# Later weight loads, paced behind compute, and LayerNorm statistics regrouped in a two-layer spectral-filter and MLP kernel

## Chip, cores, metric

One core of one Trainium2 chip. The metric is the device time of one execution in microseconds (us). PE is TensorE, DVE VectorE, ACT ScalarE, SP SyncE, POOL GpSimd. The profiles of before and after are of the fastest execution that each has (832.4 us before).

## The reference

Abridged: casts and batch handling are left out.

```python
def _A_ref(x, w_r, w_i):                       # spectral filter: B, S, D = 1, 2048, 576
    X = rfft2(x.astype(float32), axes=(-2, -1))
    X = X * (w_r + 1j * w_i)                   # w_r, w_i: 2048 x 289
    return irfft2(X, s=(S, D)).astype(bfloat16)

def _B_ref(x, w1, b1, w2, b2):                 # MLP: 576 -> 4608 -> 576
    h = gelu(einsum("bsd,df->bsf", layernorm(x), w1) + b1)
    return einsum("bsf,fd->bsd", h, w2) + b2

x = A_x
x = x + _A_ref(layernorm(x), A_w_r, A_w_i)
x = x + _B_ref(layernorm(x), B_w1, B_b1, B_w2, B_b2)
x = x + _A_ref(layernorm(x), A_w_r, A_w_i)     # the same weights again
x = x + _B_ref(layernorm(x), B_w1, B_b1, B_w2, B_b2)
```

## The kernel before

The transforms are matrix products. Per 128-row tile, stage A does fold, turn (transpose), `dft_d`, `dft_v`, then an "exchange": a DMA from SBUF to SBUF that spreads one tile over other partitions. A stage that follows needs all 16 exchanges. In the profiles, psb and pss are tiles in PSUM, where PE writes; xT, z and y1 (shown as y) are the tile after `turn`, `dft_d` and `dft_v`; v_sb, b_sb, r_sb and h_sb are large buffers in SBUF that the stages take turns in. w2 lies in v_sb and r_sb, w1 in w_sb, the GELU results in h_sb, and between two MLPs the spectral weights and the inverse transform i1 in h_sb too.

```python
    def exchange(dst, slot, src):                       # 145 KB, on SP's queue
        p0 = 32 * (slot // 4) + slot % 4
        ins = nc.sync.dma_start(out=dst[p0 : p0 + 29 : 4], in_=src).ins
        # ... (cut: declared independent of the other exchanges)

        def dft_v(self, t, on_act):
            # ... (cut: four matmuls into py)
            y1 = work.tile([P, 2, KP], BF16, tag="y1", bufs=3)
            if on_act:
                nc.scalar.copy(out=y1[:], in_=py[:, :, 0:KP])
            else:
                nc.vector.tensor_copy(out=y1[:], in_=py[:, :, 0:KP])
            exchange(self.vx, t, y1[:])

        def run_all(self):                              # stage A
            for i in range(NT + 3):
                if 0 <= i - 3 < NT:
                    self.dft_v(order[i - 3], on_act=(i % 2 == 0))
                if 0 <= i - 2 < NT:
                    self.dft_d(order[i - 2])            # PE, then z on ACT, scaled by rs
                if 0 <= i - 1 < NT:
                    self.turn(order[i - 1])             # PE, then xT on ACT
                if i < NT:
                    self.fold(order[i])                 # DVE
                    if i < 4:
                        self.stats([order[i]])          # LayerNorm statistics, DVE and a root on ACT
                    elif i % 4 == 0:
                        self.stats(order[i : i + 4])

    vx, hx = at(v_sb, [P, 16, 2, KP]), at(b_sb, [P, 16, 2, KP])
    wks, i1s = middle_tiles()             # in h_sb, with a GpSimd memset
    middle_loads(wks, i1s, True)          # f2, spectral weights, i1: issued at once
    mlp_const_loads()                     # constants, w1 (4.6 MB), w1r: issued at once
    SpectralIn(vx, sqrt=True).run_all()
    for li in range(N_LAYERS):
        last = li == N_LAYERS - 1
        middle(vx, hx, wks, i1s)
        if li == 0:
            load_w2((0, 1, 2, 3))         # 5.2 MB, as soon as v_sb and r_sb are free
            # ... (cut)
        else:
            load_w2((2, 3))
        prep = Prep(0, sqrt=li == 0)      # Newton steps on DVE where sqrt is False
        spectral_out(hx, prep)
        # ... (cut: second MLP, w2 groups 0 and 1)
            mlp(li, prep, SpectralIn(vx, sqrt=False))
            wks, i1s = middle_tiles()
            middle_loads(wks, i1s, False)
```

## Time and profile before

| | before |
|---|---|
| time, median | 836.2 us (832.4 to 838.0, 16 runs) |
| span of the profiled execution | 830.6 us |
| PE busy | 750.9 us, 90% |
| stages A to H | 72.2, 35.2, 33.3, D and E together 330.4, 28.5, 35.4, 295.6 us |

The two page lines on which the theory rests are the DMA share of 40 equal slices (in tenths) and what the engines moved, kernel before:

```profile
DMA  9951640000000000000001644300000000000000
GB/s 299 350 131 52 189 159 1 1 1 8 15 1 8 17 8 1 8 15 8 1 8 51 171 110 148 115 1 1 22 8 1 8 23 0 2 15 16 1 8 22
```

A slice is 20.8 us: the first two are saturated with loads and lie wholly in stage A.

### The profile page before, as it was taken

How to read it: one execution, taken by the hardware profiler on the slowest of the kernel's cores; microseconds unless marked ns; L12 is line 12 of the kernel's file. 1: busy time of each engine (PE TensorE's matmuls, PEld its weight loads, DVE VectorE, ACT ScalarE, POOL GpSimd, SP SyncE). 2: the span in 40 equal slices, each digit the busy share in tenths (PEclk: the TensorE clock that was granted, in tenths of full speed). 3: DMA queues.
4: the chain of work that ended last, by engine and by line, in shares of the span. 5: the costliest groups of instructions: out<-in, count | busy, mean ns of one | idle time of the engine just before them, and what ended most of it. 6: DMA issues, size and time to landing. Idle time of an engine off the chain costs nothing.

```text
span 830.6 us, 12285 instructions
## 1 busy us (share of the span) xinstructions
PE 750.9 (90%) x5121; PEld 460.9 (55%) x5121; DVE 275.4 (33%) x905; ACT 331.7 (40%) x514; POOL 37.5 (5%) x61
## 2 busy tenths in 40 slices
PE   6556569999999999999999477999999999999998
PEld 4334245358636853784378245535853773585376
DVE  6334559204611460242024476920140122020001
ACT  5435534642354235424532274354035205502510
POOL 6300000000000000000002200000000000000000
PEclk9868889999999999999999698899999999999999
DMA  9951640000000000000001644300000000000000
GB/s 299 350 131 52 189 159 1 1 1 8 15 1 8 17 8 1 8 15 8 1 8 51 171 110 148 115 1 1 22 8 1 8 23 0 2 15 16 1 8 22
DMA packets 18504, 41.59 MB, mean 50 GB/s; under 512 B 1796, under 2 KB 12880, under 8 KB 17936
## 3 DMA queue, kind: packets, MB, share of 16 engines
q0 software_dynamic: 6464, 27.88, 10.7%
q1 hardware_dynamic: 11584, 12.46, 5.3%
q8 instruction: 40, 0.66, 0.3%
q10 hardware_dynamic: 400, 0.47, 0.2%
q14 instruction: 16, 0.13, 0.0%
HBM read 28.93 MB, written 2.36 MB: 38 GB/s over the span
## 4 chain that ended last, share of the span: by engine, by line
PE 78%; DVE 10%; DMA 9%; ACT 2%; issue 1%; SPq 0%; DVEq 0%; ACTq 0%
PE psb L510 34%; PE psb L484 31%; DMA v_sb<-y 5%; PE psb L490 5%; PE psb L289 2%; DMA b_sb<-r_sb 2%; DVE tt L432 2%; PE psb L396 1%; DVE r_sb L359 1%; DVE r_sb L360 1%; DVE x_sb L433 1%; PE pss L472 1%; DVE x_sb L434 1%; DVE stats L234 1%; DVE r_sb L361 1%
## 5 line engine op out<-in xcount | busy, mean ns | idle before, releaser
L484 PE MATMUL psb<-yT,w_sb 128*128 128x512 bf16 x1152 | 261.2, 380 | 1.7 <-DVE x_sb L434 1.0
L510 PEld LDWEIGHTS <-h_sb 128*128 128x128 bf16 x2304 | 223.1, 98 | 58.2 <-issue 3.4
L497 ACT ACTIVATE h_sb<-psb,b_sb 128x512 bf16<-128x512 f32 x288 | 174.5, 688 | 197.1 <-PE psb L490 197.1
L484 PEld LDWEIGHTS <-w_sb 128*128 128x128 bf16 x1152 | 107.3, 98 | 148.8 <-issue 28.8
L510 PE MATMUL psb<-r_sb,h_sb 128*128 128x288 bf16 x1280 | 168.9, 286 | 0.0
L510 PE MATMUL psb<-v_sb,h_sb 128*128 128x288 bf16 x1024 | 133.7, 286 | 0.0
L518 DVE TENSOR_TENSOR x_sb<-psb,xb 128x576 bf16<-128x576 f32 x32 | 24.2, 758 | 259.7 <-PE psb L510 259.7
L462 DVE TENSOR_SCALAR xn<-x_sb,mv,rs 128x576 bf16<-128x576 bf16 x32 | 13.9, 433 | 195.0 <-PE pss L472 138.8
L474 ACT COPY yT<-pss 128x640 bf16<-128x640 bf16 x32 | 22.1, 692 | 71.3 <-PE pss L472 71.3
L234 DVE BATCH_NORM_STATS2 stats<-x_sb 128x6 f32<-128x288 bf16 x128 | 50.5, 436 | 0.0
L490 PE MATMUL psb<-yT,w1r_sb 64*128 64x512 bf16 x288 | 43.6, 381 | 0.0
L294 ACT ACTIVATE z<-psb,rs 128x580 bf16<-128x580 f32 x32 | 29.4, 917 | 35.2 <-PE psb L289 33.3
L281 ACT COPY xT<-pss 96x768 bf16<-96x768 bf16 x32 | 25.1, 785 | 43.7 <-PE pss L279 43.7
L289 PE MATMUL psb<-c_fd,xT 96*128 96x290 bf16 x192 | 35.2, 327 | 2.3 <-ACT xT L281 2.3
L310 ACT CAST y<-psb 128x580 bf16<-128x580 f32 x24 | 15.4, 642 | 50.1 <-PE psb L307 33.4
L426 PE MATMUL psb<-c_gd,u 128*128 128x288 bf16 x128 | 26.8, 302 | 8.2 <-ACT u L401 5.4
L432 DVE TENSOR_TENSOR tt<-psb,x_sb 128x576 f32<-128x576 f32 x32 | 24.0, 751 | 25.1 <-PE psb L426 24.8
L304 PE MATMUL psb<-z,c_k 128*128 128x290 bf16 x32 | 9.9, 311 | 23.4 <-ACT z L294 23.4
L371 PE MATMUL psb<-r_sb,h_sb 128*128 128x290 bf16 x128 | 23.9, 298 | 6.4 <-DVE r_sb L361 3.1
L289 PEld LDWEIGHTS <-xT 96*128 96x128 bf16 x192 | 20.2, 110 | 12.7 <-ACT xT L281 5.2
L350 ACT CAST r_sb<-psb 128x580 bf16<-128x580 f32 x32 | 20.8, 649 | 14.0 <-PE psb L348 12.7
L373 ACT CAST r_sb<-psb 128x580 bf16<-128x580 f32 x32 | 20.6, 644 | 13.9 <-PE psb L371 7.0
(75 smaller groups left out, 509.5 us busy)
## 6 DMA issues: line engine op xcount, KB each, us to landing
r_sb<-in_B_w_dram POOLq DMA_DIRECT2D x4, 1440.0 KB, 8.2
w_sb<-in_B_w_dram POOLq DMA_DIRECT2D x4, 1152.0 KB, 14.2
v_sb<-in_B_w_dram POOLq DMA_DIRECT2D x4, 1152.0 KB, 8.7
h_sb<-const_i POOLq DMA_DIRECT2D x8, 384.0 KB, 8.9
v_sb<-y SPq DMA_DIRECT2D x16, 145.0 KB
b_sb<-r_sb SPq DMA_DIRECT2D x16, 145.0 KB
b_sb<-y SPq DMA_DIRECT2D x16, 145.0 KB
v_sb<-r_sb SPq DMA_DIRECT2D x16, 145.0 KB
```

The source lines that it names most:

```text
L234: nc.vector.bn_stats(out=stats[:, h, :], in_=x_sb[:, t, h * DH : (h + 1) * DH])
L281: nc.scalar.copy(out=xT[:], in_=pt[0:96])
L289: nc.tensor.matmul(pz[:, o, 0:KP], lhsT=xT[:, 3 * o + ci, :], rhs=c_fd[:, 3 * o + ci, :], start=(ci == 0), stop=(ci == 2),)
L294: nc.scalar.activation(out=z[:].rearrange("p r (j o) -> p r o j", o=2), in_=pz[:, :, 0:KP].rearrange("p o (r j) -> p r o j", r=2), func=AC ...
L371: nc.tensor.matmul(ph[:, o, 0:KP], lhsT=i1[:, n % 4, pl, :], rhs=xp[:, ri, :], start=(q == 0), stop=(q == 1))
L426: nc.tensor.matmul(po[:, o, 0:DH], lhsT=lhsT, rhs=c_gd[0 : (98 if q == 2 else 128), 3 * o + q, :], start=(q == 0), stop=(q == 2),)
L432: nc.vector.tensor_tensor(out=tt[:], in0=po[:, 0:1, 0:DH].to_broadcast([P, 2, DH]), in1=xr, op=ALU.add)
L484: nc.tensor.matmul(phs[q // 2][:, q % 2, :], lhsT=w1_sb[:, ci, (fg + q) * 128 : (fg + q + 1) * 128], rhs=yT[:, ci, :], start=(ci == 0), st ...
L490: nc.tensor.matmul(phs[q // 2][:, q % 2, :], lhsT=w1r_sb[rows, (fg + q) // 2, :], rhs=yT[rows, 4, :], start=False, stop=True,)
L497: nc.scalar.activation(out=ht[:], in_=phs[q // 2][:, q % 2, :], func=ACT.Gelu_apprx_tanh, bias=b1_sb[:, fc : fc + 1], scale=1.0)
L510: nc.tensor.matmul(po[:, h, 0:DH], lhsT=hts[fc][:, i * 128 : (i + 1) * 128], rhs=w2_chunk[fc][:, h * DH : (h + 1) * DH], start=(fc == 0), ...
L518: nc.vector.tensor_tensor(out=xr, in0=po[:, :, 0:DH], in1=xb[:], op=ALU.add)
```

## The change

Its intent: keep bulk loads from competing with exchanges, by loading each tensor only shortly before it is needed and tying each load to an instruction that marks progress; and take small waits out of the statistics. In stage E an extra root on a constant (`warm`) brings ACT's table in early.

```diff
+    def load(out, in_, behind=None):
+        ins = nc.gpsimd.dma_start(out=out, in_=in_).ins
+        if behind is not None:
+            tc.add_manual_dep(ins, marks[behind].name, SYNC, reason="pace of the loads")
 ...
-            nc.gpsimd.memset(wk[:, :, :, KP - 1 : KP], 0.0)      # in both layers
+        nc.vector.memset(wk[:, :, :, KP - 1 : KP], 0.0)          # once
 ...
-            y1 = work.tile([P, 2, KP], BF16, tag="y1", bufs=3)
+            y1 = work.tile([P, 2, KP], BF16, tag="y1", bufs=5)   # f32w: 3 to 2 buffers
 ...  run_all: statistics tile by tile, root for every pair; one load per step
-                    if i < 4:
-                        self.stats([order[i]])
-                    elif i % 4 == 0:
-                        self.stats(order[i : i + 4])
+                    ln_bn_one(mv[:, i % 2, :], t)
+                    if i % 2 == 1:
+                        for tt, (_, rs) in zip(order[i - 1 : i + 1], ln_scale(mv, False, self.sqrt)):
+                            self.st["rs", tt] = rs
+                for call in loads.get(i, ()):
+                    call()
 ...  spectral_out
             if n == 2:
-                prep.stats()
+                prep.bn()
+            if n == 3:
+                prep.scale()
 ...  end of the first MLP (stage E)
             spec.fold(prev)
-            spec.stats([prev])
+            warm = work.tile([P, 1], F32, tag="ln_v")
+            nc.scalar.activation(out=warm[:], in_=c_eps[:, 0:1], func=ACT.Sqrt)
             spec.turn(prev)
+            spec.sqrt = True
+            spec.stats([prev])
 ...  the schedule of the loads
-    middle_loads(wks, i1s, True)
-    mlp_const_loads()
-    SpectralIn(vx, sqrt=True).run_all()
+    SpectralIn(vx, sqrt=True).run_all(paced)      # x, f2, w, i1: one behind each tile's xT copy
 ...
-            load_w2((0, 1, 2, 3))
+            load(c_r1[:], const_ap("r1"), ("xp", 1))                 # constants in stage B
+            # ... (cut: gd, b1, b2 likewise)
+            # w1 in three batches behind output tiles of stage C (cut)
+            # (cut, too: weights and i1 interleaved in h_sb, w1 loaded in halves of its columns)
-        prep = Prep(0, sqrt=li == 0)
+        prep = Prep(0, sqrt=True)
+        w2_loads = [lambda b, g=g: load_w2(g, b) for g in (0, 1, 2, 3)]  # behind the first GELU groups
+            for j in range(4):                                        # spectral weights again, stage E
+                b = ("y1", order[-1]) if j >= 2 else None
```

More of the change, by code (lines that the diff above doesn't have):

```diff
@@ L30 @@
 SLOT_ROWS = [8 * (4 * (p // 32) + p % 4) + (p // 4) % 8 for p in range(128)]
+SYNC = mybir.DependencyInfo(mybir.DependencyClass.Sync, mybir.DependencyReason.DATA)
 ENGINES = [getattr(mybir.EngineType, n) for n in ("PE", "Activation", "DVE", "Pool")]
@@ L188 @@
         nc.vector.memset(b[:], 0.0)
-    for j in range(1, 4):
-        nc.gpsimd.dma_start(out=x_sb[:, j::4, :], in_=xv[:, j::4, :])
-    def middle_tiles():
-        wks = [at(h_sb, [P, 4, 2, 296], j * 2368) for j in range(4)]
-        i1s = [at(h_sb, [P, 4, 3, P], 4 * 2368 + j * 1536) for j in range(4)]
-        for wk in wks:
-            nc.gpsimd.memset(wk[:, :, :, KP - 1 : KP], 0.0)
-        return wks, i1s
-    def middle_loads(wks, i1s, with_f2):
-        for j in range(4):
-            if with_f2:
-                nc.gpsimd.dma_start(out=c_f2[:, j::4], in_=f2_ap[:, j::4])
-            for ri, w_ap in enumerate((A_w_r, A_w_i)):
-                wv = w_ap.rearrange("(c e) k -> c e k", e=16)
-                nc.gpsimd.dma_start(out=wks[j][:, :, ri, 0 : KP - 1], in_=wv[:, j::4, :])
-            nc.gpsimd.dma_start(out=i1s[j][:], in_=i1_ap[:, j::4])
@@ L208, in mlp_const_loads @@
-    def mlp_const_loads():
-        nc.gpsimd.dma_start(out=c_r1[:], in_=const_ap("r1"))
-        nc.gpsimd.dma_start(out=c_gd[:], in_=const_ap("gd"))
-        nc.gpsimd.dma_start(out=b1_rows[:], in_=B_b1.rearrange("(fc p) -> fc p", p=128))
-        nc.gpsimd.dma_start(out=b2_bc[:], in_=B_b2.partition_broadcast(P))
-        for ci in range(4):
-            nc.gpsimd.dma_start(out=w1_sb[:, ci, :], in_=B_w1[ci * 128 : (ci + 1) * 128, :])
+    marks = {}
+    def load(out, in_, behind=None):
+        ins = nc.gpsimd.dma_start(out=out, in_=in_).ins
+        if behind is not None:
+            tc.add_manual_dep(ins, marks[behind].name, SYNC, reason="pace of the loads")
@@ new lines, in load_x, with load_w @@
+    def load_x(j, behind=None):
+        load(x_sb[:, j::4, :], xv[:, j::4, :], behind)
+    load_x(1)
+    GROUP = 4 * 592 + 4 * 384
+    wks = [at(h_sb, [P, 4, 2, 296], j * GROUP) for j in range(4)]
+    i1s = [at(h_sb, [P, 4, 3, P], j * GROUP + 4 * 592) for j in range(4)]
+    for wk in wks:
+        nc.vector.memset(wk[:, :, :, KP - 1 : KP], 0.0)
+    def load_w(j, ri, behind=None):
+        wv = (A_w_r, A_w_i)[ri].rearrange("(c e) k -> c e k", e=16)
+        load(wks[j][:, :, ri, 0 : KP - 1], wv[:, j::4, :], behind)
@@ L215, in mlp_const_loads, with load_i1, load_f2, load_w1 @@
+    def load_i1(j, behind=None):
+        load(i1s[j][:], i1_ap[:, j::4], behind)
+    def load_f2(j, behind=None):
+        load(c_f2[:, j::4], f2_ap[:, j::4], behind)
+    def load_w1(ci, h, behind):
+        cols = slice(h * F_FF // 2, (h + 1) * F_FF // 2)
+        load(w1_sb[:, ci, cols], B_w1[ci * 128 : (ci + 1) * 128, cols], behind)
+    def load_w1r(h, behind):
         rest = B_w1[512:576, :].rearrange("d (j two p) -> d two j p", two=2, p=128)
-        for h in range(2):
-            nc.gpsimd.dma_start(out=w1r_sb[64 * h : 64 * h + 64], in_=rest[:, h])
+        load(w1r_sb[64 * h : 64 * h + 64], rest[:, h], behind)
@@ L221, with load_w2, ln_bn, ln_bn_one @@
     w2_chunk = [w2_parts[g][:, fc - w2_first[g]] for g in range(4) for fc in range(w2_first[g], w2_first[g + 1])]
-    def load_w2(groups):
-        for g in groups:
-            rows = B_w2[w2_first[g] * 128 : w2_first[g + 1] * 128, :]
-            nc.gpsimd.dma_start(out=w2_parts[g], in_=rows.rearrange("(fc p) d -> p fc d", p=128))
-    def ln_stats(tiles, mlp, sqrt):
-        n = len(tiles)
-        mv = work.tile([P, n, nc.vector.BN_AGGR_DIM], F32, tag="ln_mv", bufs=4)
-        for i, t in enumerate(tiles):
-            stats = work.tile([P, 2, nc.vector.BN_STATS_DIM], F32, tag="ln_stats")
-            for h in range(2):
-                nc.vector.bn_stats(out=stats[:, h, :], in_=x_sb[:, t, h * DH : (h + 1) * DH])
-            nc.vector.bn_aggr(out=mv[:, i, :], in_=stats[:])
+    def load_w2(g, behind):
+        rows = B_w2[w2_first[g] * 128 : w2_first[g + 1] * 128, :]
+        load(w2_parts[g], rows.rearrange("(fc p) d -> p fc d", p=128), behind)
+    def ln_bn(tiles):
+        mv = work.tile([P, len(tiles), nc.vector.BN_AGGR_DIM], F32, tag="ln_mv", bufs=4)
+        for i, t in enumerate(tiles):
+            ln_bn_one(mv[:, i, :], t)
+        return mv
+    def ln_bn_one(mv, t):
+        stats = work.tile([P, 2, nc.vector.BN_STATS_DIM], F32, tag="ln_stats")
+        for h in range(2):
+            nc.vector.bn_stats(out=stats[:, h, :], in_=x_sb[:, t, h * DH : (h + 1) * DH])
+        nc.vector.bn_aggr(out=mv, in_=stats[:])
+    def ln_scale(mv, mlp, sqrt):
+        n = mv.shape[1]
         rs = work.tile([P, n], F32, tag="ln_rs", bufs=4)
@@ L270, in stats @@
         def stats(self, tiles):
-            for t, (_, rs) in zip(tiles, ln_stats(tiles, mlp=False, sqrt=self.sqrt)):
+            for t, (_, rs) in zip(tiles, ln_scale(ln_bn(tiles), False, self.sqrt)):
                 self.st["rs", t] = rs
@@ L280, in turn @@
             xT = work.tile([96, 6, P], BF16, tag="xT")
-            nc.scalar.copy(out=xT[:], in_=pt[0:96])
+            marks["turn", t] = nc.scalar.copy(out=xT[:], in_=pt[0:96]).ins
             self.st["xT", t] = xT
@@ L307, in dft_v, with run_all @@
             nc.tensor.matmul(py[:, 1, 0:KP], lhsT=c_k1[:, 1, :], rhs=z[:, 0, :], start=False, stop=True)
-            y1 = work.tile([P, 2, KP], BF16, tag="y1", bufs=3)
+            y1 = work.tile([P, 2, KP], BF16, tag="y1", bufs=5)
             if on_act:
-                nc.scalar.copy(out=y1[:], in_=py[:, :, 0:KP])
+                ins = nc.scalar.copy(out=y1[:], in_=py[:, :, 0:KP]).ins
             else:
-                nc.vector.tensor_copy(out=y1[:], in_=py[:, :, 0:KP])
+                ins = nc.vector.tensor_copy(out=y1[:], in_=py[:, :, 0:KP]).ins
+            marks["y1", t] = ins
             exchange(self.vx, t, y1[:])
-        def run_all(self):
+        def run_all(self, loads):
             for i in range(NT + 3):
@@ L323, in run_all @@
                 if i < NT:
-                    self.fold(order[i])
-                    if i < 4:
-                        self.stats([order[i]])
-                    elif i % 4 == 0:
-                        self.stats(order[i : i + 4])
+                    t = order[i]
+                    self.fold(t)
+                    if i % 2 == 0:
+                        mv = work.tile([P, 2, nc.vector.BN_AGGR_DIM], F32, tag="ln_mv", bufs=4)
+                    ln_bn_one(mv[:, i % 2, :], t)
[4 more added lines that the diff above has]
+                    call()
     exchanged = {}
@@ L361, in weigh @@
             nc.vector.tensor_sub(out=xp[:, 0, :], in0=ma[:, 0, :], in1=mb[:, 1, :])
-            nc.vector.tensor_add(out=xp[:, 1, :], in0=ma[:, 1, :], in1=mb[:, 0, :])
+            marks["xp", n] = nc.vector.tensor_add(out=xp[:, 1, :], in0=ma[:, 1, :], in1=mb[:, 0, :]).ins
             st["xp", n] = xp
@@ L384, with spectral_out @@
     cnt = [0]
-    def spectral_out(hx, prep):
+    def spectral_out(hx, prep, loads):
         st = {}
@@ L429, in idft_k @@
                         )
-                tt = work.tile([P, 2, DH], F32, tag="f32w", bufs=3)
+                tt = work.tile([P, 2, DH], F32, tag="f32w", bufs=2)
                 xr = x_sb[:, t, :].rearrange("p (h n) -> p h n", h=2)
@@ L433, in idft_k @@
                 nc.vector.tensor_tensor(out=xr[:, 0], in0=tt[:, 0], in1=po[:, 1, 0:DH], op=ALU.add)
-                nc.vector.tensor_tensor(out=xr[:, 1], in0=tt[:, 1], in1=po[:, 1, 0:DH], op=ALU.subtract)
+                marks["out", t] = nc.vector.tensor_tensor(out=xr[:, 1], in0=tt[:, 1], in1=po[:, 1, 0:DH], op=ALU.subtract).ins
         for n in range(9):
@@ L448, in spectral_out @@
                 prep.turn(n - 4, "act")
+            for call in loads.get(n, ()):
+                call()
     class Prep:
@@ L455, in stats, with bn, scale @@
         def stats(self):
-            self.mr = ln_stats(self.quad, mlp=True, sqrt=self.sqrt)
+            self.bn()
+            self.scale()
+        def bn(self):
+            self.mv = ln_bn(self.quad)
+        def scale(self):
+            self.mr = ln_scale(self.mv, True, self.sqrt)
             self.yT = work.tile([P, 5, 512], BF16, tag="yT", bufs=1, name=f"yT{uid()}")
@@ L476, in turn, with mlp_up @@
                 nc.vector.tensor_copy(out=self.yT[:, :, i * 128 : (i + 1) * 128], in_=pt[:])
-    def mlp_up(yT):
+    def mlp_up(yT, loads=()):
         hts = []
+        loads = list(loads)
         for fg in range(0, NFC, 4):
@@ L496, in mlp_up @@
                 ht = at(h_sb, [P, 512], 512 * fc)
-                nc.scalar.activation(
+                marks["ht", fc] = nc.scalar.activation(
                     out=ht[:], in_=phs[q // 2][:, q % 2, :], func=ACT.Gelu_apprx_tanh, bias=b1_sb[:, fc : fc + 1], scale=1.0
-                )
+                ).ins
                 hts.append(ht)
+            if loads:
+                loads.pop(0)(("ht", fg))
         return hts
     def mlp_down(t, i, hts, store, between):
-        xb = work.tile([P, 2, DH], F32, tag="f32w", bufs=3)
+        xb = work.tile([P, 2, DH], F32, tag="f32w", bufs=2)
         xr = x_sb[:, t, :].rearrange("p (h n) -> p h n", h=2)
@@ L520, in mlp_down, with mlp @@
             nc.sync.dma_start(out=ov[:, t, :], in_=x_sb[:, t, :])
-    def mlp(li, prep, spec):
+    def mlp(li, prep, spec, loads):
         prev = None
@@ L525, in mlp @@
         for q in range(4):
-            hts = mlp_up(prep.yT)
+            hts = mlp_up(prep.yT, loads if q == 0 else ())
             if q < 3:
@@ L549, in mlp @@
             spec.fold(prev)
+            warm = work.tile([P, 1], F32, tag="ln_v")
+            nc.scalar.activation(out=warm[:], in_=c_eps[:, 0:1], func=ACT.Sqrt)
+            spec.turn(prev)
+            spec.sqrt = True
             spec.stats([prev])
-            spec.turn(prev)
             spec.dft_d(prev)
             spec.dft_v(prev, on_act=True)
+    first = [("x", 2), ("x", 3)]
+    for j in range(4):
+        first += [("f2", j), ("wr", j), ("wi", j), ("i1", j)]
+    calls = {"x": load_x, "f2": load_f2, "i1": load_i1, "wr": lambda j, b: load_w(j, 0, b), "wi": lambda j, b: load_w(j, 1, b)}
+    paced = {}
+    for n, (kind, j) in enumerate(first):
+        i = 1 + max(n - 1, 0)
+        if i <= NT:
+            paced.setdefault(i, []).append(lambda kind=kind, j=j, i=i: calls[kind](j, ("turn", order[i - 1])))
+        else:
+            paced.setdefault(i, []).append(lambda kind=kind, j=j, i=i: calls[kind](j, ("y1", order[i - 3])))
     vx, hx = at(v_sb, [P, 16, 2, KP]), at(b_sb, [P, 16, 2, KP])
-    wks, i1s = middle_tiles()
-    middle_loads(wks, i1s, True)
-    mlp_const_loads()
-    SpectralIn(vx, sqrt=True).run_all()
+    SpectralIn(vx, sqrt=True).run_all(paced)
     for li in range(N_LAYERS):
@@ L563 @@
         middle(vx, hx, wks, i1s)
+        out_loads = {}
         if li == 0:
-            load_w2((0, 1, 2, 3))
+            load(c_r1[:], const_ap("r1"), ("xp", 1))
+            load(c_gd[:], const_ap("gd"), ("xp", 3))
+            load(b1_rows[:], B_b1.rearrange("(fc p) -> fc p", p=128), ("xp", 5))
+            load(b2_bc[:], B_b2.partition_broadcast(P), ("xp", 5))
             b1p = sm_ps([P, NFC])
@@ L568 @@
             nc.vector.tensor_copy(out=b1_sb[:], in_=b1p[:])
-        else:
-            load_w2((2, 3))
-        prep = Prep(0, sqrt=li == 0)
-        spectral_out(hx, prep)
+            t0, t1, t2, t3 = (("out", QUADS[q][1]) for q in range(4))
+            out_loads = {
+                1: [lambda: load_w1(0, 0, t0), lambda: load_w1(1, 0, t0), lambda: load_w1(2, 0, t0), lambda: load_w1(3, 0, t0), lambda: load_w1r(0, t0), lambda: load_w1r(1, t0)],
+                3: [lambda: load_w1(0, 1, t1), lambda: load_w1(1, 1, t1)],
+                5: [lambda: load_w1(2, 1, t2), lambda: load_w1(3, 1, t2)],
+            }
+        prep = Prep(0, sqrt=True)
+        spectral_out(hx, prep, out_loads)
+        w2_loads = [lambda b, g=g: load_w2(g, b) for g in (0, 1, 2, 3)]
         if last:
-            load_w2((0, 1))
-            mlp(li, prep, None)
+            mlp(li, prep, None, w2_loads)
         else:
             vx, hx = at(b_sb, [P, 16, 2, KP]), at(v_sb, [P, 16, 2, KP])
-            mlp(li, prep, SpectralIn(vx, sqrt=False))
-            wks, i1s = middle_tiles()
-            middle_loads(wks, i1s, False)
+            mlp(li, prep, SpectralIn(vx, sqrt=False), w2_loads)
+            for j in range(4):
+                b = ("y1", order[-1]) if j >= 2 else None
+                load_w(j, 0, b)
+                load_w(j, 1, b)
+                load_i1(j, b)
 _INS = ['A_x', 'A_w_r', 'A_w_i', 'B_x', 'B_w1', 'B_b1', 'B_w2', 'B_b2']
```

## The prediction

> **What bounds the kernel now.** I read the page first, then cut the span at the seams between stages and asked the windows view for one row per stage (busy microseconds of each engine, number of instructions, granted clock, DMA share, GB/s):
>
> ```profile
> 0.00:72.20 72.20, 41.10 (x257) 27.45 (x258) 29.54 (x99) 32.61 (x48) 20.75 (x37) 0.85 0.75 233
> 72.20:107.30 35.10, 21.62 (x129) 12.20 (x129) 20.82 (x65) 19.13 (x32) 2.31 (x3) 0.79 0.47 136
> 107.30:140.70 33.40, 27.17 (x245) 20.21 (x246) 27.00 (x64) 15.48 (x21) 1.38 (x2) 0.89 0.27 89
> 140.70:458.20 317.50, 316.00 (x2172) 193.25 (x2172) 96.53 (x390) 131.91 (x202) 6.05 (x12) 1.00 0.04 11
> 458.20:471.10 12.90, 2.67 (x17) 1.50 (x18) 3.23 (x17) 2.35 (x3) 3.39 (x5) 0.68 0.86 241
> 471.10:499.60 28.50, 21.60 (x128) 12.31 (x129) 20.62 (x64) 19.25 (x32) 0.96 (x1) 0.86 0.34 87
> 499.60:535.00 35.40, 28.58 (x244) 20.55 (x245) 28.83 (x75) 15.40 (x20) 2.72 (x3) 0.84 0.39 131
> 535.00:830.60 295.60, 292.12 (x1932) 173.45 (x1932) 48.88 (x134) 95.54 (x156) 0.00 (x0) 1.00 0.03 11
> ```
>
> I call the rows A to H: A is the first spectral input, B the middle, C the spectral output, D the first MLP with the second layer's spectral input woven in, E the tail of that input, F and G middle and output of layer two, H the second MLP. D and H, 613 us of 831, are PE at 99% and full clock. No part of this change makes that shorter; everything to be had lies in the other 217 us. There A has a DMA share of 0.75 and PE busy only 57%. B and F run the same program and differ by 6.6 us; C and G run nearly the same and differ by 2.0 us. Those two differences are the first hint.
>
> Then the chain of work that ended last, where a DMA is the longest piece of a stage:
>
> ```profile
> 10.64 9.61 DMA v_sb<-y
> 21.00 12.75 DMA v_sb<-y
> ...
> 34.62 17.50 DMA v_sb<-y
> ...
> 69.14 2.79 DMA v_sb<-y
> ...
> 91.95 10.86 DMA b_sb<-r_sb
> ...
> 103.58 3.52 DMA b_sb<-r_sb
> ```
>
> ```profile
> 464.76 6.07 DMA b_sb<-y
> ...
> 496.56 2.81 DMA v_sb<-r_sb
> ```
>
> These are the 145 KB exchanges that move one tile between partitions. The same transfer takes 2.8 us on a quiet memory system and 6 to 17.5 us when bulk loads are in flight. The waits view says who pays in A: the copies that fill y1, whose three buffers are freed only when an exchange has landed.
>
> ```profile
> DVE y L312 <- DMA v_sb<-y: 17.5, 3, 9.5
> ...
> ACT y L310 <- DMA v_sb<-y: 16.5, 4, 9.2
> ```
>
> So 34 us of waits in A stand behind exchanges. After 55 us, when the loads are done, the timeline shows the pace without them, one tile per start of z (2.62 us):
>
> ```profile
> 61.58 0.91 ACT L294 ACTIVATE z<-psb,rs 128x580 bf16<-128x580 f32 x1 [1.07 <-PE psb L289]
> ...
> 64.20 0.91 ACT L294 ACTIVATE z<-psb,rs 128x580 bf16<-128x580 f32 x1 [0.32 <-PE psb L289]
> ```
>
> **What the Trainium skill says.** "DMA: Bandwidth & Descriptors", section Queues, rings and completion order: each DMA engine takes turns between the queues that have work, a packet at a time. Exchanges (SyncE's queue) and loads (GpSimd's) thus share the engines; the trace agrees, 9.61 to 17.50 us against 2.79. "TensorE: Matmul & The Clock Gate", Part 1: PE falls to half clock after about 3.4 us idle and needs about that much work to come back. The trace agrees: the L304 matmul at 29.84 follows 3.48 us of idling and takes 0.40 to 0.45, and 0.28 again from 33.48; the first return to full clock, at 19.28, comes much later than 3.4 us after the first matmul. "ScalarE: Activation LUTs", section What ACT_TABLE_LOAD costs: about 1283 ns; the trace has 1.28 us at 144.68, ahead of the first GELU.
>
> **The change part by part.** The order of instructions, before against after, is identical on PE and SyncE. What moves is when GpSimd issues loads, plus some LayerNorm work on DVE and ACT.
>
> *Paced loads and five y1 buffers, stage A.* The MLP's weights and constants leave A: four of 1152 KB, two of 288, then 432, 144 and 128, 5.9 MB. What stays, 7.7 MB of x, f2, spectral weights and i1, is issued one load per tile. At 290 to 384 KB per 2.65 us this is about 125 GB/s, with the exchanges (145 KB per tile, 55 GB/s) 180, against the 273 to 383 of A's first 40 us. Exchanges should then take 3 to 4 us, and five buffers at 2.65 us cover 13 us. A becomes the latency chain z (0.92), dft_v (0.65), dft_d (0.92) and hand-over. Its start stays cold: before, dft_v of tiles 0 to 3 begins at 8.43, 12.01, 15.64 and 19.28, 3.6 us apart, and I keep that. From 19.28 on, 12 more tiles. I take 2.67 instead of 2.62, because ACT now has a square root for every pair of tiles (0.29 us) ahead of a y1 copy, in a gap of 1.65 us that already holds 0.78 of xT and 0.64 of y1. Last dft_v: 19.28 + 12 x 2.67 = 51.3. From there to the first dft_u was 67.78 to 72.18, 4.4 us, which gives 55.7. **A saves 16.5 us.**
>
> *The w2 loads go from B to the first MLP.* The two long exchanges at the end of B, 10.86 and 3.52, stand beside w2 loads issued at 90.66 and 93.41. Without them B should look like F, 28.5. **B saves 6.6 us.** In the MLP, 5.2 MB issued behind the first four groups of GELU need some 17 us at 300 GB/s, and the first use comes 37.7 us after the MLP's start: hidden.
>
> *w1 goes into C.* 5.2 MB in three batches behind output tiles, the first about 6.5 us into C, leaves 26 us. It takes about 17 and touches no exchange: hidden. C itself is DVE from the first addition at 112.48 to 143.49: 16 tiles x 1.52, four statistics of 0.93, four norms of 0.6, 31 us with almost no gap. Moving the square root one step later frees ACT (its u copy sat behind a 6.43 us wait), so PE's 3.5 us gap there shrinks, but DVE is the bound, so I give only the 0.36 us that DVE waited for the root. **C saves 0.4.**
>
> *Square root instead of Newton steps in G.* In G twelve small DVE operations run from 514.84 to 517.05, 2.2 us inside a DVE-bound stretch. **G saves 2.2.** In return the GELU table has to be loaded again at H: in D it made the second group of up-matmuls late (140.67 to 149.72 is 9.05 us, against 8.26 in H before). **H loses 0.8.**
>
> *Stage E.* Statistics of the last tile: Newton ends at 461.85, while dft_d's matmuls end near 460.98. With a root and a reciprocal, about 0.7 us after the aggregate at 459.67, z starts when PE is done: 1.0 us. The table load for it falls into ACT's 2.66 us gap before xT. Half of the spectral weights' loads no longer wait for a memset and go out a few microseconds earlier; the other half waits for the last y1 copy, so it leaves at the same moment as the last exchange. I put that exchange at 3.8 us, between 2.8 and the 6.07 of now: 2.3 us. **E saves 3.3.**
>
> Sum: 16.5 + 6.6 + 0.4 + 2.2 + 3.3 - 0.8 = 28.2 us. Span 830.6 - 28.2 = 802.4; from the median, 836.2 - 28.2 = 808.0. The profiled run was the fastest of five (832.42, 1.8 above its span), and the 5 us spread probably comes from the contended stages, which the change calms, so I lean one down: **807 us**.
>
> **The rivals.** (1) *A stays slow for another reason.* ACT's order binds harder than I assume: the root waits for DVE's statistics of the same step, as a wait of 6.43 us did in C. For: DVE now does 3.7 us per pair of tiles in a period of 5.3, and in odd steps its y1 copy comes ahead of the statistics. Against: that leaves 1.6 us of slack. At 3.0 us per tile A ends 4 us later: 811. If PE never got warm there, 3.6 us per tile, it would end 11 us later: 818. (2) *The contention only moves.* Loads that are now late hold up C or the first MLP, or the last exchange of E still takes 6 us. For E this speaks: the release by the same copy. It costs 2.3 us: 809. A late w1 or w2 would show as a PE wait on w_sb or v_sb; there are 9 and 20 us of slack. (3) *PE warms earlier than 19.28 in A*, because fewer waits break up its work: up to 3 x 1.0 us better: 804. (4) *The loads were hidden anyway*, and removing them exposes only a chain of equal length. Against: the quiet pace of 2.62 was seen in this very stage.
>
> **Range and chances.** The working has one large term, A, which I trust to about 5 us either way, and several of 1 to 2 us. 799 to 816 covers rivals 1 (at 3.0), 2 and 3. Two per cent is 819.5; to miss it, A would have to give less than a third of its gain. Faster 0.93, same 0.06, slower 0.01.
>
> **What would show it right or wrong.** First dft_u near 55.7 with z starts 2.6 to 2.7 apart and no y1 wait on an exchange; B at 28.5, with last exchanges of about 3 us; C near 33 and DVE-bound; no PE wait on w_sb, v_sb or r_sb in D; E at 9.6; G at 33.2; a table load at the start of H with a gap under 1 us; D unchanged at 317.5. Wrong would be: y1 copies still waiting for exchanges, tiles 3 us apart behind sq, PE at half clock through A, or a gap in PE before the first down-projection.

## More of the kernel before

The stages are named in the prediction. In the results I cut them at fixed instructions, and leave D and E in one piece: A ends at the first `dft_u` matmul, B at the first matmul of `idft_v_rest`, C at the first up-matmul, and so on.

## The result, and the profile after

The median is 801.7 us (799.7 to 804.8, 9 runs) against 836.2 (16 runs): ratio 0.960, 95% interval 0.958 to 0.962, faster. A ratio is the mean time of one kernel's fast runs over that of the other's of the same rounds, so it is not quite the ratio of the medians. The profiled span is 797.3, 33.3 less than before.

The windows view of the kernel after, one row per stage as in the prediction (A to H):

```profile
0.00:53.60 53.60, 33.21 (x256) 22.52 (x257) 30.38 (x104) 33.67 (x50) 14.62 (x23) 0.99 0.70 201
53.60:82.40 28.80, 21.78 (x131) 12.43 (x133) 20.73 (x65) 19.00 (x32) 2.18 (x4) 0.86 0.38 109
82.40:115.10 32.70, 27.32 (x244) 20.18 (x245) 26.83 (x64) 16.73 (x22) 6.00 (x10) 0.89 0.50 163
115.10:431.90 316.80, 315.88 (x2172) 193.31 (x2172) 96.64 (x390) 132.22 (x204) 8.18 (x10) 1.00 0.10 31
431.90:441.00 9.10, 2.67 (x16) 1.45 (x17) 1.56 (x6) 2.54 (x4) 3.22 (x5) 0.64 0.24 66
441.00:469.20 28.20, 21.13 (x129) 11.77 (x130) 20.44 (x64) 19.19 (x32) 1.23 (x2) 0.92 0.50 143
469.20:502.60 33.40, 27.74 (x249) 20.27 (x250) 27.66 (x65) 16.78 (x22) 0.00 (x0) 0.91 0.00 1
502.60:797.30 294.70, 291.19 (x1929) 173.00 (x1927) 48.01 (x133) 95.54 (x156) 3.68 (x4) 1.00 0.08 27
```

The eight durations show where the gain lies: A, B, E and G. (These seams were set by eye; the one ahead of H is 0.9 us past the first up-matmul, at 501.67, where the table below cuts.) In A the granted clock (third number from the end) went from 0.85 to 0.99, and the bytes per second from 233 to 201 GB/s in a much shorter stage. The chain of work that ended last still holds the exchanges, but as short pieces:

```profile
49.47 3.88 DMA v_sb<-y
...
79.32 2.80 DMA b_sb<-r_sb
```

and further on in the same view:

```profile
437.52 3.27 DMA b_sb<-y
...
466.16 2.79 DMA v_sb<-r_sb
```

In place of three long exchanges in A (39.9 us of the chain before) there is one, the last. The slow start of PE ends at the second tile, at 11.81, where before it ended at the fourth, at 19.28 (timeline, first `dft_v` matmul of a tile: 0.40 us at the low clock, 0.28 at the full):

```profile
8.24 0.40 PE L316 MATMUL psb<-z,c_k 128*128 128x290 bf16 x1 [0.69 <-ACT z L306]
...
11.81 0.28 PE L316 MATMUL psb<-z,c_k 128*128 128x290 bf16 x1 [0.41 <-ACT z L306]
```

Stage A can be accounted for by the starts of its 16 z instructions. Before, they ran from 7.46 to 66.82: 15 steps of 2.6 us would be 39.0; three long steps (5.4, 5.6, 11.3) add 14.5 and six steps at PE's low clock (3.3 to 3.6) add about 6. After, they run from 7.28 to 47.15: 14 steps of 2.59 and one of 3.57. Three of the six slow steps before are the cold start, the other three each follow one of the long waits. So the waits for exchanges were most of the loss in A, and the low clock, a good part of it brought on by the waits, was the rest.

The same cuts for predicted and measured, in us:

| stage | before | predicted change | after | measured change |
|---|---|---|---|---|
| A | 72.2 | -16.5 | 53.6 | -18.6 |
| B | 35.2 | -6.6 | 28.7 | -6.4 |
| C | 33.3 | -0.4 | 32.8 | -0.6 |
| D and E | 330.4 | -3.3 | 325.9 | -4.5 |
| F | 28.5 | 0 | 28.2 | -0.4 |
| G | 35.4 | -2.2 | 32.5 | -2.9 |
| H | 295.6 | +0.8 | 295.6 | 0.0 |
| sum | 830.6 | -28.2 | 797.3 | -33.3 |

### The profile page after: what moved, and what is told of

The parts are those of the page before. It is cut to its first block, busy times and chain, and to the rows that moved or that the text cites. A ratio compares the mean times of both kernels' runs of the same rounds, so it can differ in the third digit from the quotient of the medians.

```text
span 797.3 us, 12262 instructions
## 1 busy us (share of the span) xinstructions
PE 740.9 (93%) x5121; PEld 454.9 (57%) x5121; DVE 272.3 (34%) x888; ACT 335.7 (42%) x521; POOL 39.1 (5%) x57
## 4 chain that ended last, share of the span: by engine, by line
PE 81%; DVE 12%; ACT 3%; DMA 2%; issue 1%; DVEq 0%; SPq 0%; ACTq 0%
PE psb L542 36%; PE psb L514 32%; PE psb L520 5%; PE psb L301 3%; DVE tt L450 2%; ACT z L306 2%; DVE x_sb L451 2%; DVE r_sb L378 2%; DVE r_sb L377 2%; DVE x_sb L452 1%; DVE r_sb L379 1%; PE psb L316 1%; DVE r_sb L380 1%; PE pss L501 1%; DVE stats L243 1%
## 5 line engine op out<-in xcount | busy, mean ns | idle before, releaser
L301 PE MATMUL psb<-c_fd,xT 96*128 96x290 bf16 x192 | 30.9, 298 | 1.8 <-ACT xT L293 1.8
L450 DVE TENSOR_TENSOR tt<-psb,x_sb 128x576 f32<-128x576 f32 x32 | 23.9, 748 | 17.8 <-PE psb L444 17.8
L520 PEld LDWEIGHTS <-w1r_sb 64*128 64x128 bf16 x288 | 8.2, 94 | 30.5 <-issue 30.5
L301 PEld LDWEIGHTS <-xT 96*128 96x128 bf16 x192 | 18.0, 100 | 11.2 <-ACT xT L293 6.2
```

Source lines behind the costliest of these rows:

```text
L301: nc.tensor.matmul(pz[:, o, 0:KP], lhsT=xT[:, 3 * o + ci, :], rhs=c_fd[:, 3 * o + ci, :], start=(ci == 0), stop=(ci == 2),)
L450: nc.vector.tensor_tensor(out=tt[:], in0=po[:, 0:1, 0:DH].to_broadcast([P, 2, DH]), in1=xr, op=ALU.add)
L520: nc.tensor.matmul(phs[q // 2][:, q % 2, :], lhsT=w1r_sb[rows, (fg + q) // 2, :], rhs=yT[rows, 4, :], start=False, stop=True,)
```

## The experiments

Theory at the outset: exchanges slowed by loads in flight make A and B long; the change helps by pacing the loads, with five buffers as reserve. Rivals: the buffers alone do it; the volume moved out of A alone does it; the statistics do it. Runs named `b_` start from the kernel before, runs named `a_` from the kernel after. A stage's length is read from one profiled execution. The two kernels with identical stage A programs, before and `b_w2late`, had 72.2 and 76.9 there, so in unpaced kernels a stage A of one profile is good to about 5 us only; the times over several rounds weigh more. (In b_w2late PE was at its low clock for the last six tiles, from 53.88 on, in before for one tile after the last long wait.) The profiles of b_w1late and b_w2late are also of the slowest of their four runs, so that their stages understate the gain.

### b_y1x5: before, five y1 buffers

```diff
-            y1 = work.tile([P, 2, KP], BF16, tag="y1", bufs=3)
+            y1 = work.tile([P, 2, KP], BF16, tag="y1", bufs=5)
 # and f32w 3 to 2 buffers, without which it does not fit
```

> The kernel before with one part of the change alone: five y1 buffers in place of three (and f32w 3 to 2 to make room). Loads stay unpaced. Theory (pacing): with 330 GB/s of loads in flight an exchange takes 6 to 17 us whatever the buffers, so more buffers let more exchanges queue but the last of them still land when the loads are through; stage A (to the first dft_u) shrinks by at most 6 us of 18.6, time near 831. Rival (buffers): with 5 in place of 3 exchanges in flight the throughput rises to 5/3 and the copies hardly wait; A ends at 60 or earlier, time near 823 or less. B unchanged at 35 in both.

Measured: 831.8 us, ratio 0.995 (0.992 to 0.999); A 70.2. Buffers alone give about 4 us, against 35 for the whole change. The chain and the timeline of this run say why not more:

```profile
28.24 24.53 DMA v_sb<-y
```

```profile
54.38 0.40 PE L304 MATMUL psb<-z,c_k 128*128 128x290 bf16 x1 [9.34 <-ACT z L294]
...
58.01 0.40 PE L304 MATMUL psb<-z,c_k 128*128 128x290 bf16 x1 [0.42 <-ACT z L294]
```

Five exchanges queue in place of three, and the one that blocks takes 24.5 us. After the wait PE is at its low clock, and here it stays there: 3.6 us from tile to tile up to the last at 65.29, though PE paused only 0.42 to 1.06 us ahead of the groups that follow.

### b_w1late: before, only w1 moved behind the second output tile of C

```diff
-            nc.gpsimd.dma_start(out=w1_sb[:, ci, :], in_=...)            # stage A
+            d = nc.gpsimd.dma_start(out=w1_sb[:, ci, :], in_=...).ins    # called in stage C
+            tc.add_manual_dep(d, marks["out", QUADS[0][1]].name, SYNC, ...)
```

> The kernel before with only the four w1 loads (4.6 MB) moved out of A, behind the second output tile of C; three buffers, unpaced, w2 as before. Theory (volume): A's loads end some 14 us earlier (4.6 MB at 330 GB/s), A ends near 60 instead of 72, time near 824. Rival (pacing alone counts): three buffers still stall under the unpaced remainder, A ends within 4 us of before, time 832 and up. If w1 comes too late for the first MLP, PE waits on w_sb there.

Measured: 821.1 us, ratio 0.983 (0.980 to 0.986), so 14 us by the ratio; A 62.9. PE has no wait on w_sb in the first MLP. That is the largest single part of the gain, without pacing and with three buffers. No run moves the other 1.3 MB that the change takes out of A (constants and w1r) alone; their share is not known. Two long exchanges remain in its chain, both while the remaining loads run:

```profile
13.88 10.60 DMA v_sb<-y
...
25.37 10.17 DMA v_sb<-y
...
59.86 2.79 DMA v_sb<-y
```

### b_w2late: before, only the first layer's w2 moved into the first MLP

```diff
-            load_w2((0, 1, 2, 3))
+            if w2_groups:                          # in mlp_up, first quad of layer one
+                load_w2_behind(w2_groups.pop(0), first)
```

> The kernel before with only the first layer's w2 loads moved from the end of B to the first MLP. Theory: B becomes as long as the second middle, 35.1 to 28.5, and nothing else changes; time near 829.6 (6.6 less). Rival: the gain is given back in the first MLP, which would show as a PE wait on v_sb or r_sb there and a time near 836.

Measured: 828.8 us, ratio 0.991 (0.988 to 0.994), 7.3 us; B 28.6, as F. The end of B in its chain, where before had 10.86 and 3.52:

```profile
102.46 2.79 DMA b_sb<-r_sb
```

No PE wait on v_sb or r_sb appears in the first MLP. The prediction's step for B stands.

### a_unpaced and a_y1x3: after, one guard of A taken off

```diff
-    SpectralIn(vx, sqrt=True).run_all(paced)
+    for kind, j in first:                       # a_unpaced
+        calls[kind](j, None)
+    SpectralIn(vx, sqrt=True).run_all({})
```

```diff
-            y1 = work.tile([P, 2, KP], BF16, tag="y1", bufs=5)
+            y1 = work.tile([P, 2, KP], BF16, tag="y1", bufs=3)      # a_y1x3
```

> The kernel after with the loads of stage A issued all at once ahead of the loop; w1, w2 and constants stay late, five buffers stay. Theory (pacing): 7.7 MB at 330 GB/s saturate the DMA engines for the first 25 us; exchanges of that time take 6 to 10 us, five buffers (13 us) swallow nearly all of it, and A ends 1 to 4 us later than after: 803 to 806. If pacing itself is what counts: A ends 8 us or more later, 810 and up. If only the volume counts: same as after within 1 us.

> The kernel after with three y1 buffers again. Theory (pacing): paced exchanges take 3 to 4 us, and three buffers at 2.6 us per tile cover 7.8 us, so nothing is lost: within 1 us of after (802). Rival (buffers): A becomes longer again by 5 us or more (807 and up), with y1 copies waiting for exchanges in the waits view.

Measured: 800.8 us without pacing (ratio 0.959, 0.957 to 0.961; A 53.9) and 800.7 with three buffers (0.959, 0.956 to 0.961; A 54.5). Neither differs from after. For a_unpaced I had expected 1 to 4 us more; instead five buffers swallow the slow exchanges almost whole. Its chain has one of 12.66 us, and the only y1 copy that waited for an exchange waited 0.4 us:

```profile
16.72 12.66 DMA v_sb<-y
```

In a_y1x3 no y1 copy waited for an exchange. Pacing, which I had put first, is not needed where there are five buffers, and five buffers are not needed where there is pacing.

### a_unp3_Eearly: both guards off, and E's loads released early

```diff
 # both edits above, and in stage E:
-                b = ("y1", order[-1]) if j >= 2 else None
+                b = None
```

> The kernel after with both of A's guards off (loads unpaced and three y1 buffers), and, in stage E alone, the second half of the spectral weights' loads released as soon as their memory is free. Each guard alone could be taken off for nothing. Theory (either guard is enough): together they matter; three buffers cover 7.8 us and the exchanges beside 7.7 MB of unpaced loads take 6 to 10, so A becomes 56 to 61 long instead of 53.6 to 55. Rival (only the volume counts): A stays at 54 to 55. E: in after these loads leave with the last exchange, which took 3.3 us; released early they are through before it or just overlap: D and E together within 1 us of 325.9. If they collide as in before (6.07 us): 328 or more.

Measured: 808.3 us (803.4 to 811.4), ratio 0.967 (0.964 to 0.970); A 58.4 in the profile, which was of the fastest of the six runs. Against after's 0.960 that is 0.7% or about 6 us: the two guards stand in for each other, and one of them is needed. The waits view shows the y1 copies behind exchanges again:

```profile
DVE y L324 <- DMA v_sb<-y: 6.4, 2, 4.2
```

Stage E is independent of this: D and E together are 325.4, 0.5 less than after. All twelve loads were issued by 436.3, the exchange began at 441.95 and took the quiet time:

```profile
441.95 2.78 DMA b_sb<-y
```

So holding half of the loads back (3.27 us after) is no better than letting them go early. In the kernel before, the twelve loads went out from 452.68, up to 461.6, because the GpSimd memset ahead of them had to wait for h_sb, and the exchange at 464.76 met them. (The change also puts weights and i1 of a group side by side in h_sb; no run separates this from the memset.)

### a_quad_Enewton: after, A's statistics per four tiles, and Newton steps in E

```diff
-                    ln_bn_one(mv[:, i % 2, :], t)          # and the root per pair
+                    if i < 4:
+                        self.stats([order[i]])
+                    elif i % 4 == 0:
+                        self.stats(order[i : i + 4])
 # stage E: no warm, stats with sqrt False
```

> The kernel after with A's LayerNorm statistics in groups of four tiles as before, and, in stage E alone, Newton steps for the last tile in place of the root. A: b_w1late left A at 62.9, so some 8 us of the gain are not w1's; if the grouping has a share, A becomes longer by 1 to 5 us (z waits for rs, tiles held up behind four tiles' statistics at once, 3.7 us each); if pacing and buffers have it all, A stays at 54 to 55. E: Newton ended 1.0 us after dft_d in before, so D and E together 326.9 instead of 325.9.

Measured: 803.3 us, ratio 0.962 (0.959 to 0.965), at most 2 us above after and with overlapping intervals; A 55.3, D and E 326.6. The profile shows where the grouping costs: once, ACT's root waits for the statistics of four tiles, and that step of z takes 3.79 us in place of 2.6:

```profile
16.95 0.30 ACT L251 ACTIVATE sq<-mv,c_eps 128x4 f32<-128x4 f32 x1 [2.04 <-DVE mv L244]
```

That is about 1 us, but a_newton and a_poolmemset, with after's stage A, had 54.9 and 55.1, so neither the time nor A as a whole resolves it. In E, z starts 4.62 us after the last down-matmul, in after 3.72: the root gives 0.9, where I had 1.0; 0.7 of it is left in D and E together.

### a_newton: after, Newton steps in G

```diff
-        prep = Prep(0, sqrt=True)
+        prep = Prep(0, sqrt=li == 0)
```

> The kernel after with the Newton steps back in the first statistics of layer two's MLP (sqrt only in layer one). G was 35.4 before and 32.5 after, 2.9 less where I expected 2.2. If the root accounts for it all: G back at 35.4, time 2.9 more (804.6). If the twelve DVE operations alone count: 2.2 more (803.9), the rest being the removed loads or the split of statistics and scale. If G is not DVE-bound: no change (801.7).

Measured: 803.7 us, ratio 0.963 (0.961 to 0.966), 2 to 3 us above after, with intervals that just overlap; G 34.7, 2.2 more. The twelve DVE operations account for most of G's gain. The G of the `a_` kernels with the root ranged from 32.5 to 33.6, so the 0.7 beyond my 2.2 is within that range and not explained further.

### a_poolmemset: after, the memset on GpSimd

```diff
-        nc.vector.memset(wk[:, :, :, KP - 1 : KP], 0.0)
+        nc.gpsimd.memset(wk[:, :, :, KP - 1 : KP], 0.0)
```

> The kernel after with the memset of the weight tiles' last column on GpSimd again. In the build this makes the ACT table load ahead of the first GELU carry the wait for the first up-matmuls, as in before; after, the load carries no such wait and runs early. Theory: the load lands after the first up group, PE idles some 0.6 to 0.8 us in the first two groups of D; time 0.8 more (802.5), H unchanged. Rival (something else made D 0.8 us shorter): the first three groups start 4.1 us apart as in after.

Measured: 801.7 us, too close to after to tell apart by time; D and E 326.7 against 325.9. D alone, up to the last down-matmul, is 316.66 or 316.67 in this run, in before and in every `b_` kernel, and 315.86 to 315.88 in after and all other `a_` kernels. The timeline shows what differs. The ACT table load ahead of the first GELU, kernel before, kernel after, and this run:

```profile
144.68 1.28 ACT L497 ACT_TABLE_LOAD   x1 [5.19 <-PE psb L490]
```

```profile
113.96 1.28 ACT L527 ACT_TABLE_LOAD   x1
```

```profile
120.83 1.28 ACT L527 ACT_TABLE_LOAD   x1 [5.37 <-PE psb L520]
```

In the bracket is the idle time ahead of the instruction and who ended it. With the memset on GpSimd, the first GELU has one more engine to wait for; in the build the wait for PE then sits on the table load, which cannot start before the first up-matmuls are done, and PE idled 0.64 us for a free psb buffer in both such kernels. After, the load carries no wait for PE, runs 1.2 us ahead of the first up-matmul and costs nothing. This was a side effect of moving a memset.

### a_swap, a_order2, a_best: can A's chain be shortened?

In the kernel after, A is a chain of z, dft_v, dft_d, z at 2.59 us per tile. Three orders of emission were tried.

```diff
 # a_swap:   dft_d, dft_v, turn, fold, statistics
 # a_order2: turn, dft_d, dft_v, fold, statistics
 # a_best:   root and reciprocal of the last pair; turn, dft_d, fold, statistics, dft_v
 #           y1 copies on ACT in odd steps, on DVE in even ones; and E's loads released early
```

> A version meant to beat both: after, with dft_d of the next tile issued ahead of dft_v in stage A, so that the chain z, dft_v, dft_d, z of 2.59 us per tile is broken and ACT's own work (0.92 + 0.78 + half of 0.64 + half of 0.29, about 2.2 with hand-over 2.3) sets the pace. Expected A 4 to 5 us shorter, time near 797. Rival: PE falls cold or the three psb buffers bind, and the pace stays at 2.6: 801.7.

Measured: 814.4 us, ratio 0.976 (0.973 to 0.978): slower than after by 13 us, A 67.1. My expectation had overlooked ACT's order. The chain of this run shows the new loop; xT, which the next dft_d needs, now stands on ACT behind z and a y1 copy:

```profile
22.24 0.26 ACT z L306
...
23.01 0.62 ACT y L322
23.63 0.70 ACT xT L293
24.38 1.63 PE psb L301 x6
```

The last number, 1.63 for six matmuls that take 0.92 at full clock, shows PE at its low clock again.

> The second try to beat both: stage A emits turn, dft_d, dft_v instead of dft_v, dft_d, turn. The swap of dft_d and dft_v alone made the chain longer (A 67.1): xT then sat behind z and a y1 copy on ACT, and dft_d waited for it. With turn first, xT is made one step ahead, dft_d waits for nothing of the same step, and ACT's own 2.2 to 2.3 us per tile sets the pace: from tile 2 on 14 x 0.3 = 4 us less, A near 49.5, time near 797.5. Rival: DVE's statistics hold up the root on ACT, or PE is so lightly loaded that it falls cold: A at 54 or above.

Measured: 800.2 us, ratio 0.957 (0.955 to 0.960), A 51.8: better than a_swap by 15 us by the ratios, not clearly apart from after. DVE's order was the new limit: a fold behind a y1 copy (PE waited 1.07 us in every second step), statistics behind it as well (ACT waited 1.04).

> The third try to beat both, with what the others showed: after, with stage A emitted as turn, dft_d, fold and statistics, dft_v; the root and reciprocal of a pair one step later; y1 copies on ACT in odd and on DVE in even steps; and E's loads released early (2.78 instead of 3.27 us for the last exchange). In the order turn, dft_d, dft_v a pair of tiles took 4.8 us, of which PE waited 1.07 for a fold that sat behind a y1 copy on DVE, and ACT 1.04 for the statistics. Without these ACT's own work sets the pace, xT, z, half of y1 and half of the root, 2.2 us per tile. Expected A about 49 (51.8 with that order, 53.6 after), D and E 325.4, time near 797 to 798. Rival: another hand-over takes the place of these waits and the pace stays at 2.4 or more: A 51.5 or above, 800.

Measured: 794.7 us (793.3 to 795.1), ratio 0.952 (0.950 to 0.953), clear of after's interval: 0.9% faster than after, 4.8% faster than before. A is 48.3, the sum of D and E 326.1. The timeline of ACT shows a pair of tiles every 3.96 us, so 1.98 per tile, less than my 2.2 because neighbouring ACT instructions overlap by about 0.1:

```profile
24.91 0.92 ACT L306 ACTIVATE z<-psb,rs 128x580 bf16<-128x580 f32 x1
...
28.87 0.92 ACT L306 ACTIVATE z<-psb,rs 128x580 bf16<-128x580 f32 x1
```

At that pace all z are done by 39, and yet A ends at 48.3. The chain has the reason, and it is the old one:

```profile
31.75 9.39 DMA v_sb<-y
...
42.01 6.03 DMA v_sb<-y
```

The loads are tied to the tiles, so faster tiles call for loads faster: the DMA share in 20 to 40 us is 0.89 to 0.90. The next microseconds lie in fewer bytes ahead of A's end (i1, for instance, is first used some 3 us into B), which I have not tried.

## Why the prediction was right, point by point

**The size.** 807 predicted, 801.7 measured; the gain was 34.5 where I had 29.2. The time is in the range but nearer its lower end.

**A, mechanism.** "The MLP's weights and constants leave A" was the right part to name and carries most of it: w1 alone 14 us. I named pacing and five buffers in one breath with it. The runs separate them: singly neither is worth anything in the changed kernel, together they are worth 6 us. The 34 us of waits that I counted are those of DVE and ACT added together, and not what A lost by them: that was the 14.5 us of the three long steps and the slow clock after each. The waits for exchanges did vanish as foretold (one of 2.28 us, ending at 46.19, is still put down to an exchange, but the matmuls that this copy needs had ended 0.04 us before it), and with them three steps at PE's low clock that each followed a long wait. My sentence that the trace agrees with the 3.4 us of idling that cost PE its clock was too smooth: in the same trace the matmul at 39.07 follows 3.62 us of idling and still takes 0.28, and the slow ones come within the next microsecond.

**A, size.** The step that failed is "Its start stays cold ... and I keep that". PE was at full clock from the second tile, not the fourth; from 19.28 to 17.00 for the fourth tile is 2.3 us. My rival 3 named this and put it at up to 3 us, but its reason, fewer waits, is not borne out, and these 2.3 us are in part luck. b_w2late, with before's stage A, had the full clock with the second tile as well (at 12.19); a_newton, with after's stage A, with the third; a_unpaced with the third, a_unp3_Eearly with the fifth. It changes from profile to profile of one and the same stage A, and what decides it I cannot say from these profiles. The pace was 2.59, not 2.67 (0.9 us over 12 tiles): the root on ACT fits into the gap, so rival 1 did not happen. The last leg took 5.5 instead of 4.4 us, a loss of 1.1, its exchange 3.88 long. Sum: 2.3 + 0.9 - 1.1 = 2.1, as measured.

**B and w2.** 6.6 predicted, 6.4 in the profile, 7.3 by b_w2late alone. Nothing was given back in the MLP, so rival 2 did not happen there, nor for w1 in C.

**C.** 0.4 predicted, 0.6 measured, and C of the `a_` kernels varied from 32.6 to 33.5: no more than agreement.

**E.** 3.3 predicted, 3.7 measured: the exchange 3.27 instead of the assumed 3.8, the root 0.9.

**G.** 2.2 predicted, 2.9 measured, 2.2 in the profile of a_newton.

**H and D.** "H loses 0.8" was wrong, and D, which I had left unchanged, gained 0.8. I had put D's late second group down to the table load as such. a_poolmemset shows that it was the wait the load carried; with that wait gone both MLPs start without loss.

**Rival 4**, that the loads were hidden anyway, is refuted by b_w1late.

**The sum of the parts**, by differences of ratios times 836: w1 14, w2 7, the two guards 6, G 3, and from profiles E 4 and D 1, together 35 against a measured 33 by the ratio. So no large part is unaccounted for, though these terms are not independent measurements of one kernel and each is good to 1 to 3 us.

## What to carry to other kernels

A small transfer that a chain waits for is delayed by everything queued around it, so first count the bytes that are in flight then and need not be; moving a bulk load to a stage that makes no such transfers is worth more than pacing it or buffering around it. Long waits cost twice where PE loses its clock. When a stage is reordered, write down the order on every engine: an order that frees PE can put ACT or DVE in series, as a_swap did, and once the order is right, the transfers can be the limit again.

## What the Trainium skill lacked or had wrong

- "TensorE: Matmul & The Clock Gate", Part 1, gives about 3.4 us of sustained activity as the price of the full clock, with some 0.5 us of variation, and warns that the number of slow matmuls differs from run to run. Here, in streams with pauses and with transposes among the matmuls, it took from the first matmul to the first fast `dft_v` 8.3 us (after), 15.7 (before) and 19 (a_unp3_Eearly), and in b_y1x5 PE had not come back between 54.38 and 65.29, 11 us, with pauses of 0.42 to 1.06 us ahead of the groups in between (in b_w2late, 18 us from 53.88). Nor was the loss tied to 3.4 us of idling: after 2.26 us in a_unp3_Eearly (at 29.47) the next matmul took 0.40, after 3.62 in before (at 39.07) 0.28. What counts as activity was not separated by any run.
- "DMA: Bandwidth & Descriptors", Queues, rings and completion order, says that queues take turns, but not what this does to a short transfer beside a long backlog. From issue to landing, the 145 KB exchange took 2.8 us alone, 3.0 to 4.7 with loads at after's pace, 9.4 beside loads at a DMA share of 0.9, up to 17.8 beside the backlog of before's stage A, and 24.5 with five exchanges in flight. Earlier exchanges of the same queue can be part of these times; no run separates them from the loads.
- "ScalarE: Activation LUTs", What ACT_TABLE_LOAD costs: the 1283 ns agree (1.28 us each time). The further 1380 ns of drain, for 2.66 in all, do not show here: before, the load ran from 144.68 to 145.96 and the first GELU began at 145.98; after, it began 0.02 us after the copy ahead of it had ended (113.94). In stage E of after both sides are tight: the copy ends at 430.21, the load runs from 430.23 to 431.51, and the root begins at 431.52.
- No page that I read says that a table load can carry the waits of the activation behind it, and so run late. Here that decided whether PE lost 0.6 to 0.8 us.
